# Segment 3's memory asked inside the attention, and the fallback flag ahead of the last halvings

## The chip, the cores and the metric

The kernel runs on one core of a Trainium2 chip. The metric is the device time of one execution in microseconds; a shorter time is better. The engines are TensorE (PE, with its weight loads shown apart as PEld), VectorE (DVE), ScalarE (ACT), GpSimd (POOL) and SyncE (SP, which here mainly issues DMAs). Work passes through SBUF, matmul results through the PSUM banks.

## The reference

Two attentions over 2048 tokens with a width of 576 and 32 heads of 18, whose outputs stand side by side. A has one key and one value head for all its query heads. B works in four segments of 512 tokens: a causal softmax inside the segment, and beside it a memory M, z of all the earlier segments, which is asked with phi(q).

```
phi = lambda t: jnp.where(t > 0, t + 1.0, jnp.exp(t))
# A
p = softmax(einsum("bhqd,bkd->bhqk", q, k) * Dh ** -0.5);  o = einsum("bhqk,bkd->bhqd", p, v);  out_A = o @ wo
# B, for s in range(4)
a_dot = einsum("bhqk,bhkd->bhqd", softmax(qs @ ks * scale + mask), vs)
num = einsum("bhld,bhde->bhle", phi(qs), M)
den = einsum("bhld,bhd->bhl", phi(qs), z)[..., None] + 1e-6
o = g * num / den + (1.0 - g) * a_dot          # g = sigmoid(beta), by head
M = M + einsum("bhld,bhle->bhde", phi(ks), vs);  z = z + sum over l of phi(ks)
out_B = concat of all o, @ wo
```

## The kernel before

**Projections.** The first stage computes q, k and v, A's first and then B's segments one by one (`for s in range(NSEG)`). A projection splits its fp32 operands into a high and a low part and adds the three products that matter: 14 matmuls of 512 columns for one part of 126 rows (`proj`, L249), and 14 of 288 or 306 columns for 128 tokens of v (`values`, L491). Parts t = 0 to 4 cover the 576 columns. q and k are then halved again (`split2`, a cast on ACT at L118 and a subtraction on DVE at L119) and stored to DRAM; v goes to DRAM through `vch`, copied by ACT (L493) and stored from ACT's DMA queue (L496, `vB`). The engines' order in this stage is set by a scheduler, within what `hold` and `pin` fix.

For each part of q in segments 1 to 3 `phi` (L382 to L389) runs a Relu and an Exp on ACT (L385, L386) and one max-and-add on DVE (L388). `from_memory(t)` (L423) then does one of two things. For a segment that is not in `LATE_ASK` it multiplies with the memory of the earlier segments on PE (L429), scales by the gate on DVE (L433) and stores `numB` (L434). For a segment in `LATE_ASK` it only stores phi(q) to `qfB` (L426). The denominators are formed in the same loop for segments that are not in `LATE_ASK`: five matmuls with `zst` (L545), 1e-6 added on DVE (L549), a store of `denB` (L550). `LATE_ASK` is (1, 2), so segment 3 asks inside its projections.

The scores' softmax has no running maximum; a bound for every query is subtracted instead. The bound's products stand at L554, its maximum in `fm` at L555, its halves in `shift_parts`. In the last segment `loose_flag` (L391 to L400) reduces all bounds to one number (a reduction on DVE, a transpose on PE at L396, another reduction, a comparison, a cast) and writes `flag`, which is 1 if a bound is too loose for fp32. The flag is loaded into registers of all engines (L606), and a branch (L607) leads either to a slow block, which isn't taken with these inputs, or past it. SP waits in the branch for DMAs that are still under way.

**Attention.** From there on a schedule written out by hand sets the order on PE, ACT and DVE (`tc.manual_schedule`). It is a list of 416 turns of three score items each (two, once in a block of A). An item is one tile of keys for two heads: matmuls into a PSUM tile `E` (L925 for A, L934 for B), an exp on ACT into `P` (L943), for one item of three by way of a copy `W` on DVE (L940); for some items of A the exp is computed on DVE (L898 to L908). The products with v, `O` (L973), follow two turns behind. A block of A has 11 turns, a block of B two; after each of the first blocks of A come two or four blocks of B. Between scores and products a turn has a place for one other piece of PE work:

- while `ask_memory` lasts (from turn k = 20 on, `ASK`), a step of it in turns whose items are all of A: four matmuls of 256 columns (L827), 12 steps to a segment, with the scaling (L832), the 1e-6 (L836) and stores of `numB` and `denB` behind them. The memories of all late segments are loaded together from `mzB` into the tile of A's output weights (L810), the phi(q) of one segment by `load_qf` (L802) into one of two "o" tiles;
- once it has ended, one step of an output projection: `run_fill(1)`, eight matmuls of 192 columns (L770). What isn't done by the last turn is done behind it, in the tail (L1133 on).

Loads, sums, inverses, weightings and stores hang on a list of due turns (`at`, `due`): `finish` begins a block's sums, `place()` (L1056) tells when the parts of another block may take an "o" tile: fewer than two in use, and the late segments asked so far at least `min(2, len(parts) + 1)`. Stacks of queries and keys (`stA`, `stB`, L138, L139) come by SP's queue two ahead.

Of the kernel before, what the change touches and what calls it, by code (L numbers as in the profile page):

```python
# [54 lines left out]
CA = 618  # L55
MZ = 126 + 32

LATE_ASK, ASK = (1, 2), 20


def below(rows, r0):
# [10 lines left out]
def attention_pair_kernel(ctx, tc, a_xT, a_w, a_wo, b_xT, b_w, b_wo, b_beta, ident_d, hmask_d, bmask_d, cmask_d, sel_d, zmask_d, selx_d, sely_d, out):  # L72
    nc = tc.nc
# [40 lines left out]
    def split2(pool, src, R, hold=lambda ins: ins):  # L114

        n = src.shape[-1]
        qp = pool.tile([128, 2, C], F32R, name="qp", bufs=3)
        hold(nc.scalar.copy(qp[:R, 0, :n], src))  # L118
        hold(nc.vector.tensor_tensor(qp[:R, 1, :n], src, qp[:R, 0, :n].bitcast(F32), op=ALU.subtract))  # L119
        return qp  # L120
# [32 lines left out]
    with ExitStack() as ph:  # L153
# [30 lines left out]
        pin = tc.keep_in_program_order  # L184
# [217 lines left out]
        for s in range(NSEG):  # L402
# [15 lines left out]
            def magnitude(t, pj):  # L418
                R = RT[t]
                aqs[t] = p2.tile([128, C], BF, name="aq", bufs=5)  # L420
                nc.scalar.activation(aqs[t][:R], pj[:R], AF.Abs)

            def from_memory(t):  # L423
                R = RT[t]
                if s in LATE_ASK:
                    nc.sync.dma_start(qfB[s][:R, t], fs[t][:R])  # L426
                    return
                pn = ps.tile([128, C], F32, name="mm", bufs=1)
                nc.tensor.matmul(  # L429
                    pn[:R], Mst[:R, t].rearrange("p h d -> p (h d)")[:, :R], fs[t][:R], start=True, stop=True  # L430
                )
                nm = p2.tile([128, C], F32, name="nm", bufs=2)
                nc.vector.tensor_scalar(nm[:R], pn[:R], gt[:R, t : t + 1], None, op0=ALU.mult)  # L433
                nc.sync.dma_start(numB[s][126 * t : 126 * t + R], nm[:R])  # L434
# [88 lines left out]
            if not last:  # L523
                for i in range(4):
                    values(i, 1)

            for t in range(4):
                pj = ps.tile([128, C], F32, name="pj", bufs=4)
                proj(pj[:126], wBh, wBl, xh, xl, 126 * t, 126)
                magnitude(t, pj)  # L530
                qp = split2(pt, pj[:126], 126)
                store_parts(qp, 0, 126, qB[s], 7 * t, 7)
                if s == 0:
                    nx[2](t, behind=True)
                    if t == 3:
                        nx[2](4, behind=True)
                if s:
                    fs[t] = phi(pj[:126], 126, "qf", 5)
                    from_memory(t)
# [15 lines left out]
            nc.vector.tensor_reduce(fm[:, 1 + s : 2 + s], pu, axis=AX.X, op=ALU.max)  # L555
            if last:
                loose_flag()
            sp = shift_parts(pt, pu, -BOUND_UP, C, 128)
            sent = nc.sync.dma_start(shB[s].rearrange("j r t -> r j t"), sp.bitcast(F32))
            if last:  # L560
# [241 lines left out]
    def load_qf(s):  # L802
        qfs[s] = pa.tile([128, 5, C], F32, name="o", bufs=2)
        nc.sync.dma_start(qfs[s][:126, :4], qfB[s][:126, :4])
        nc.sync.dma_start(qfs[s][: RT[4], 4], qfB[s][: RT[4], 4])
# [210 lines left out]
    def at(k, cost, ready, step):  # L1016
        later.append((k, cost, ready, step))
        later.sort(key=lambda e: e[0])
# [15 lines left out]
    def finish(k, ab, c, hg):  # L1034

        ts = range(4) if hg == 6 else range(4, 5)
        lo, hi = (0, 28) if hg == 6 else (28, 32)
        box, need = {}, 3 if ab == "B" and c > 0 else 1
        weighed.setdefault((ab, c), 0)
        last = (ab, c) == blocks[-1][:2]  # L1040

        d0, d1, d2, d3 = (0, 2, 0, 3) if last else (2, 5, 3, 5) if (ab, c) == ("B", 0) else (2, 5, 3, 6)

        def begin(k):
            assert ab == "A" or c not in LATE_ASK or asked[0] >= c
            summing.add(hg)
            box[0] = sums(ab, c, lo, hi)
            at(k + d1, 0, lambda: True, inv)

        def inv(k):  # L1050
            inverses(ab, c, lo, hi, box[0])
            summing.remove(hg)
            for t in ts:
                at(k, 0, place, lambda k, t=t: load(k, t))

        def place():  # L1056

            return (ab, c) in parts or len(parts) - filled[0] // FILL < 2 and asked[0] >= min(2, len(parts) + 1)

        def load(k, t):  # L1060
            load_heads(ab, c, t)
            at(k + d2, 0, room, lambda k: weights(k, t))

        def room():

            return loaded[0] + need <= 10

        def weights(k, t):
            loaded[0] += need
            tiles = load_inverses(ab, c, t)  # L1070
            box[t, t] = weigh(ab, c, t, tiles)
            at(k + d3, 1, lambda: True, lambda k: heads(k, t))

        def heads(k, t):
            box[t, t].pop(0)()
            if box[t, t]:
                at(k, 1, lambda: True, lambda k: heads(k, t))
                return
            loaded[0] -= need
            weighed[ab, c] += 1  # L1080
            if weighed[ab, c] == 5 and not last:
                at(k + 2, 0, lambda: True, lambda k: fill.append(out_proj(ab, c)))

        at(k + d0, 0, lambda: hg not in summing, begin)
# [8 lines left out]
    with tc.manual_schedule(engines={ENG.PE, ENG.Activation, ENG.DVE}):  # L1093

        for n, b in enumerate(blocks):
            ms = [m for m in range(len(its)) if block_of[m] == n]
            items = [(m, k) for m in ms for k in range(2)]
            for out_, cut in ((turns, len(items) // 3), (prods, len(items) // 3 - 2)):  # L1100
                at_ = split(len(items), cut)
                out_ += [items[a:z] for a, z in zip(at_, at_[1:])]
        at(ASK + 4, 0, lambda: True, lambda k: load_qf(2))
        for k in range(len(turns) + 2):
            now[0] = k
            exps = [scores(its[n], pr, i == 1) for i, (n, pr) in enumerate(turns[k])] if k < len(turns) else []
            for i in (0, 2, 1) if len(exps) == 3 else range(len(exps)):
                exps[i]()
            if memory is None:
                run_fill(1)  # L1110
            elif k >= ASK and all(its[n][0] == "A" for n, pr in turns[k]) and next(memory, None) is None:
                memory = None

            ends = k > 1 and any(hf and its[n][3] == (NKT - 1 if its[n][0] == "A" else 2) for n, hf in prods[k - 2])
            if slow and (slow[0][0] <= k or not ends):
                slow.pop(0)[2]()
            for n, hf in prods[k - 2] if k > 1 else []:
                ab, c = its[n][:2]
                hg = products(its[n][:3], its[n][3], hf)
                if hg in (6, 7):  # L1120
                    finish(k, ab, c, hg)
                if hg == 7 and ab == "B" and c + 1 < NSEG:
                    load_vseg(c + 1)
            due(k)
            for n, pr in turns[k] if k < len(turns) else []:
                it = its[n]
                ab = it[0]
                if pr == 0:
                    prefetch(ab, keys[ab].index((ab, it[1], it[2] // 2)) + 2)
                    if it in (("A", 0, 2, 8), ("A", 0, 5, 8)):  # L1130
                        load_wo(*(("B", b_wo) if it[2] == 2 else ("A", a_wo)))

        ab, c = blocks[-1][:2]  # L1133
        ending.append(True)
        while fill:
            due(k, 4)
            run_fill(8, whole=True)
            k += 1
        while weighed[ab, c] < 4:
            due(k, 4)  # L1140
            k += 1
        banks = [psE.tile([128, 2, 512], F32, name="E") for _ in range(3)]
        dst = [bk[:, hf, :288] for bk in banks for hf in range(2)]
        for nm in ("O", "F"):
            bk = psO.tile([128, C], F32, name=nm)
            dst.append(bk[:, :288])
        for g in range(8):
            for t in range(4):
                out_part(ab, c, g // 2, t, dst[g], 288 * (g % 2), 288, t == 0, False)
        while later:  # L1150
            due(k, 4)
            k += 1
        for g in range(8):
            out_part(ab, c, g // 2, 4, dst[g], 288 * (g % 2), 288, False, True)
        for i in range(4):
            osb = pp.tile([128, 2, 512], F32, name="P", bufs=PBUFS)
            for hf in range(2):
                (nc.vector.tensor_copy if hf else nc.scalar.copy)(osb[:, hf, :288], dst[2 * i + hf])
            out_store(ab, c, i, osb[:, :, :288])
# [56 lines left out]
```

## Time and profile before

| | |
|---|---|
| median of 3 runs | 1428.27 us |
| lowest and highest | 1426.28 and 1429.96 us |
| the profiled execution | 1427.14 us |
| its span, first to last instruction | 1425.4 us |
| busy in the span: PE, ACT, DVE, POOL | 1410.3, 1195.2, 1022.9, 247.0 us |
| mean granted TensorE clock | 0.997 |

"Busy" is the time in which at least one instruction of an engine ran; matmuls overlap, so PE's busy time isn't PE at its peak. The projections take the span up to about 290 us, the attention lasts to about 1376 us, and the rest is the tail. Times in rows count from the span's start. A row of a timeline or a chain starts with the time and the length in us; brackets give how long the engine sat idle before, and what released it.

### The profile page before, as it was taken

To read this page: it belongs to the slowest core of one execution; us is meant where nothing else is said; L and a number is where in the kernel's file an instruction comes from. 1 tells how busy PE (TensorE), PEld (TensorE's weight loads), DVE (VectorE), ACT (ScalarE), POOL (GpSimd) and SP (SyncE) were. 2 spreads that over 40 slices of the span, in tenths; PEclk is the share of its full clock that TensorE was granted. 3 is DMA by queue.
4 is the path that set the end of the run, shared out by engine and by line. 5 is a ranking of instruction groups with operands and counts; after the bars stand their busy time and mean duration, and the time that the engine had idled before them with its cause. 6 is when DMAs were issued, how large, how long until landed. Compare 5 with 4: busy or idle time off the path is not lost.

```text
span 1425.4 us, 41103 instructions
## 1 busy us (share of the span) xinstructions
PE 1410.3 (99%) x17692; PEld 839.5 (59%) x17692; DVE 1022.9 (72%) x1213; ACT 1195.2 (84%) x1429; POOL 247.0 (17%) x326
## 2 busy tenths in 40 slices
PE   9999999999999999999999999999999999999998
PEld 6788888755555555555555555555555555555565
DVE  6556456467787778777777888777778877877761
ACT  4543434489999999999999999999999999999960
POOL 2431000003313214131111150131013300200001
PEclk9999999999999999999999999999999999999999
DMA  9866546457564535232322532231105121110022
GB/s 275 261 215 188 168 143 226 161 165 230 158 202 159 170 109 175 87 108 77 102 68 66 175 118 86 85 114 64 36 34 151 48 78 51 51 43 18 18 87 77
DMA packets 90469, 172.71 MB, mean 121 GB/s; under 512 B 14576, under 2 KB 22377, under 8 KB 89854
## 3 DMA queue, kind: packets, MB, share of 16 engines
q1 hardware_dynamic: 83722, 159.75, 35.8%
q0 software_dynamic: 1664, 4.78, 1.3%
q10 hardware_dynamic: 4896, 5.51, 1.2%
q8 instruction: 140, 2.29, 0.7%
q14 instruction: 47, 0.39, 0.1%
HBM read 99.32 MB, written 70.67 MB: 119 GB/s over the span
## 4 chain that ended last, share of the span: by engine, by line
PE 66%; ACT 9%; issue 2%; DVE 1%; DMA 0%; POOL 0%; DVEq 0%; ACTq 0%
PE O L973 30%; PE E L925 19%; PE F L770 11%; ACT P L943 9%; PE E L934 3%; PE E L770 1%; PE F L827 1%; PE O L770 1%; DVE W L940 1%; DMA out<-osb 0%; DVE osb L795 0%; DVE q L905 0%; DVE q L902 0%; POOL P L948 0%; DVE o L832 0%
## 5 line engine op out<-in xcount | busy, mean ns | idle before, releaser
L943 ACT ACTIVATE P<-E 128x1024 f32<-128x1024 f32 (+1 forms) x800 | 783.3, 1065 | 12.1 <-PE E L925 12.0
L940 DVE COPY W<-E 128x1024 f32<-128x1024 f32 (+1 forms) x384 | 461.2, 1201 | 177.9 <-PE E L925 120.6
L973 PE MATMUL O<-P,VA 128*32 128x256 f32 x7936 | 508.5, 380 | 0.0
L943 ACT ACTIVATE P<-W 128x1024 f32<-128x1024 f32 (+1 forms) x384 | 429.1, 1117 | 2.4 <-DVE W L940 2.2
L973 PEld LDWEIGHTS O<-P,VA 128*32 128x32 f32 x7936 | 262.7, 110 | 146.5 <-issue 5.7
L925 PE MATMUL E<-stA,kstA 56*128 56x512 f32 x1920 | 328.4, 439 | 1.1 <-ACT P L943 0.4
L925 PEld LDWEIGHTS E<-stA,kstA 56*128 56x128 f32 x1920 | 154.9, 184 | 176.3 <-ACT P L943 110.2
L948 POOL TENSOR_SCALAR_AFFINE_SELECT P<-P 128x256 f32<-128x256 f32 (+1 forms) x192 | 94.6, 493 | 474.4 <-ACT P L943 441.5
L758 POOL TENSOR_TENSOR o<-o,rb 126x512 f32<-126x512 f32 (+1 forms) x55 | 81.2, 1490 | 410.7 <-PE F L770 142.2
L770 PE MATMUL F<-woB,o 126*32 126x192 f32 (+1 forms) x1920 | 127.4, 338 | 0.3 <-DVE osb L795 0.3
L905 DVE SCALAR_TENSOR_TENSOR q<-q,PD 128x1024 f32<-128x1024 f32 x96 | 119.3, 1243 | 0.0
L973 PE MATMUL O<-P,vseg 128*32 128x256 f32 (+2 forms) x1536 | 81.4, 344 | 0.0
L770 PEld LDWEIGHTS F<-woB,o 126*32 126x32 f32 (+1 forms) x1920 | 38.2, 108 | 70.8 <-issue 62.4
L770 PE MATMUL F<-woA,o 126*32 126x192 f32 (+1 forms) x1240 | 77.7, 338 | 0.6 <-DVE osb L795 0.6
L982 DVE COPY oe<-O 128x512 f32<-128x512 f32 x64 | 44.3, 692 | 42.6 <-PE O L973 41.2
L118 ACT CAST qp<-pj 126x512 fp32r<-126x512 f32 (+1 forms) x54 | 30.9, 584 | 49.9 <-DVE kmB L447 32.7
L249 PE MATMUL pj<-xh,wBl 128*126 128x512 f32 x180 | 72.3, 403 | 0.0
L249 PE MATMUL pj<-xh,wBh 128*126 128x512 f32 x180 | 71.8, 400 | 0.0
L119 DVE TENSOR_TENSOR qp<-pj,qp 126x512 fp32r<-126x512 f32 (+1 forms) x54 | 36.6, 686 | 37.3 <-ACT qp L118 37.2
L934 PE MATMUL E<-stB 56*128 56x256 f32 (+3 forms) x512 | 61.7, 348 | 1.6 <-ACT P L943 1.1
L973 PEld LDWEIGHTS O<-P,vseg 128*32 128x32 f32 x1536 | 48.8, 109 | 24.3 <-issue 1.6
L934 PEld LDWEIGHTS E<-stB 56*128 56x128 f32 x512 | 38.6, 185 | 32.0 <-ACT P L943 22.3
(182 smaller groups left out, 1366.3 us busy)
## 6 DMA issues: line engine op xcount, KB each, us to landing
stB<-kB SPq DMA_DIRECT2D x96, 144.0 KB
stB<-qB SPq DMA_DIRECT2D x32, 288.0 KB
stA<-qA SPq DMA_DIRECT2D x30, 288.0 KB
oA<-oe SPq DMA_DIRECT2D x32, 256.0 KB
oB<-oe SPq DMA_DIRECT2D x32, 256.0 KB
qA<-qp SPq DMA_DIRECT2D x16, 504.0 KB
kB<-qp SPq DMA_DIRECT2D x16, 504.0 KB
qB<-qp SPq DMA_DIRECT2D x16, 504.0 KB
```

Of the source, the lines that this page charges most:

```text
L119: hold(nc.vector.tensor_tensor(qp[:R, 1, :n], src, qp[:R, 0, :n].bitcast(F32), op=ALU.subtract))
L249: nc.tensor.matmul(dst, w[:, c0 : c0 + M], x, start=i == 0, stop=i == len(ops) - 1)
L758: return lambda: tc.keep_in_program_order(nc.gpsimd.tensor_tensor(dst, a, b, op=op))
L770: nc.tensor.matmul(dst[32 * j : 32 * j + 32], parts[ab, c][: RT[t], t, r0 : r0 + 32], wo[ab][: RT[t], t, c0 : c0 + n], start=start, stop=stop,
L905: steps.append(lambda a=a: v.scalar_tensor_tensor(q, q, a, p, op0=ALU.add, op1=ALU.mult))
L925: nc.tensor.matmul(e[:, j], kstA[rows, 128 * kt : 128 * kt + 128], st[rows, h, :], start=True, stop=True)
L934: nc.tensor.matmul(e[:, j, c0 : c0 + 512 - 128 * k], st[rows, 4 + h, ks], st[rows, h, 128 * k :], start=True, stop=True)
L940: nc.vector.tensor_copy(src[:, :, :n], e[:, :, :n])
L943: nc.scalar.activation(p[:, :, :n], src[:, :, :n], AF.Exp, scale=SCALE)
L948: nc.gpsimd.affine_select(diag, diag, pattern=[[0, 2], [0, m], [1, 128]], base=0, channel_multiplier=-1, compare_op=ALU.is_ge, fill=0.0)
L973: nc.tensor.matmul(o[32 * j : 32 * j + 32, q0 : q0 + n], v, p[:, j % 2, p0 : p0 + n], start=m == hf == 0, stop=last and hf == 1,)
L982: nc.vector.tensor_copy(osb, o)
```

## The change

`LATE_ASK` takes in segment 3. So its memory is stored to `mzB` behind segment 2, its phi(q) is stored (now on GpSimd's queue in the last segment), and its numerators and denominators come from twelve more steps of `ask_memory`. `load_qf(3)` stands at the due turn 32, once segment 1 has been asked. A step of `ask_memory` now also stands in a turn of B if the products of that turn, two behind, are of B too. `place()` waits until three segments are asked for a second block's parts. `mzB` and its load grow by half.

In the last segment the halvings, stores, phis and `from_memory` of parts 2 and 3 are kept back in `rest` and run behind `loose_flag`, pinned in that order.

```diff
-LATE_ASK, ASK = (1, 2), 20
+LATE_ASK, ASK = (1, 2, 3), 20
...
             def from_memory(t):
                 R = RT[t]
                 if s in LATE_ASK:
-                    nc.sync.dma_start(qfB[s][:R, t], fs[t][:R])
+                    (nc.gpsimd if last else nc.sync).dma_start(qfB[s][:R, t], fs[t][:R])
                     return
...
+            rest = []
             for t in range(4):
                 pj = ps.tile([128, C], F32, name="pj", bufs=4)
                 proj(pj[:126], wBh, wBl, xh, xl, 126 * t, 126)
                 magnitude(t, pj)
+                if last and t > 1:
+
+                    rest.append((t, pj))
+                    continue
                 qp = split2(pt, pj[:126], 126)
...
             if last:
                 loose_flag()
+                for t, pj in rest:
+                    qp = split2(pt, pj[:126], 126, pin)
+                    store_parts(qp, 0, 126, qB[s], 7 * t, 7)
+                    fs[t] = phi(pj[:126], 126, "qf", 5, pin)
+                    from_memory(t)
...
         def place():
 
-            return (ab, c) in parts or len(parts) - filled[0] // FILL < 2 and asked[0] >= min(2, len(parts) + 1)
+            return (ab, c) in parts or len(parts) - filled[0] // FILL < 2 and asked[0] >= min(3, len(parts) + 2)
...
         at(ASK + 4, 0, lambda: True, lambda k: load_qf(2))
+        at(ASK + 12, 0, lambda: asked[0] >= 1, lambda k: load_qf(3))
...
-            elif k >= ASK and all(its[n][0] == "A" for n, pr in turns[k]) and next(memory, None) is None:
+            elif k >= ASK and its[turns[k][0][0]][0] in ("A", its[prods[k - 2][0][0]][0]) and next(memory, None) is None:
+
                 memory = None
```

## The prediction

> **What bounds the kernel now.** I read the table of windows first, cut at the borders of stages and of blocks of turns; then the last projection stage by line, the way from it to the attention, and the chain of waits inside the attention. In the windows the columns are the stretch and its length, then busy time (and instructions) of PE, PEld, DVE, ACT and POOL, the granted clock, the DMA share and GB/s.
>
> ```profile
> 260.58:290.28 29.70, 29.70 (x148) 20.70 (x145) 15.60 (x28) 13.68 (x27) 0.00 (x0) 1.00 0.58 195
> 290.28:291.83 1.55, 0.01 (x1) 0.03 (x1) 0.00 (x0) 0.40 (x1) 0.00 (x0) 1.00 0.07 14
> 292.87:299.70 6.83, 6.08 (x37) 2.64 (x36) 6.54 (x6) 6.83 (x8) 0.43 (x1) 0.50 0.44 102
> 339.38:368.72 29.34, 29.26 (x404) 14.81 (x400) 25.13 (x26) 29.00 (x32) 1.63 (x3) 1.00 0.63 189
> 368.72:387.24 18.52, 18.06 (x260) 10.56 (x256) 11.44 (x12) 18.51 (x24) 10.19 (x22) 1.00 0.53 164
> 455.74:475.21 19.47, 19.47 (x325) 12.23 (x321) 11.41 (x14) 19.47 (x26) 10.55 (x22) 1.00 0.33 91
> 601.17:630.32 29.15, 28.86 (x405) 14.92 (x402) 23.83 (x24) 29.11 (x32) 6.54 (x4) 1.00 0.42 133
> 1373.98:1425.40 51.42, 45.91 (x920) 31.46 (x916) 8.83 (x21) 4.92 (x8) 6.37 (x5) 0.97 0.25 85
> ```
>
> The last segment's projections (first row) are bound by PE: busy for all 29.70 us. A gap of 1.55 us follows, and then the attention, where ACT is busy for 29.00 of 29.34 us in A turns with memory steps, 18.51 of 18.52 in eight B turns that carry no other PE work, and 29.11 of 29.15 in A turns with output-projection steps ("fill"). So ACT's exps set its pace, with one near exception: in eight B turns with fill, PE and ACT are both full and the stretch is 0.95 us longer. The tail (last row) is PE's. It follows that PE time taken out ahead of the attention counts in full, as far as the way into the attention shortens with it, and that PE time put into the attention costs only what sticks out beyond ACT. The program lasts 1427.14 us in this execution, 1.74 more than its span of 1425.4; the median of the runs shown, 1428.27, is 1.13 above it.
>
> **The change, part by part.**
>
> *1. Less PE work in the last segment.* With segment 3 among those asked late, its five memory products (L429) go, and so do the five products of the denominators (L545), which are computed only for segments that are asked early. The groups by line of 260.5 to 292 (busy, then mean ns of one) and two rows of the timeline:
>
> ```profile
> L429 PE MATMUL mm<-qf,Mst 126*126 126x512 f32 (+1 forms) x10 | 5.2, 602 | 0.0
> L545 PE MATMUL nd<-qf,zst 126*32 126x512 f32 (+1 forms) x10 | 3.4, 602 | 0.0
> ...
> 283.14 1.02 PE L429 MATMUL mm<-qf,Mst 126*126 126x512 f32 x2
> 284.10 1.05 PE L545 MATMUL nd<-qf,zst 126*32 126x512 f32 x4
> ```
>
> One product is two records of 602 ns. Two L429 records take 1.02, so the second starts 0.42 behind the first; four L545 take 1.05, so 0.15 apart. PE pipelines, so what a group occupies is its pitch: ten L429 at 0.42 are 4.2 us, ten L545 between 0.15 and 0.42 are 1.5 to 4.2. I take 2.3 for these (the busy 3.4 less the 0.35 to 0.45 by which each of three groups overlaps its neighbours). Together 6.5. The new order costs some of it back: by its buffers the second of the last four values products uses the PSUM bank of the first and must wait for ACT's copy of it; I put that bubble at 0.5, from the 0.40 us of such a copy (below). So PE ends the projections **6.0 us** earlier, at about 284.3 instead of 290.28 (bounds 4.5 and 7.5).
>
> The DVE scalings (L433), the +1e-6 (L549) and the stores of numB and denB go with it; none was late for PE. In their place come five stores of phi(q) on POOL's queue, which issues no other transfer there.
>
> *2. The flag.* The halvings and phis of parts 2 and 3 move behind the flag's reduction.
>
> ```profile
> L400 DVE CAST flag<-fm x1: 141/141/141, 286.5 to 286.5; 1x1 int32<-1x1 f32 x1
> L606 DVEq TENSOR_LOAD <-flag x1: 1151/1151/1151, 286.7 to 286.7; - x1
> L607 SPq EVENT_SEMAPHORE  x8: 17/17/17, 291.1 to 291.6; - x8
> ...
> L386 ACT ACTIVATE ph_e<-ph_e 126x512 f32<-126x512 f32 x3 | 1.9, 628 | 0.1
> ...
> 288.89 0.33 ACTq L496 DMA_DIRECT2D vB<-vch  x1
> 290.32 0.40 ACT L493 COPY vch<-pj 128x288 f32<-128x288 f32 x1 [1.47 <-PE pj L491]
> 291.53 0.33 ACTq L496 DMA_DIRECT2D vB<-vch  x1
> 291.83 1.17 PE L925 MATMUL E<-st,kstA 56*128 56x512 f32 x6 [1.55 <-SPq L607]
> 292.57 1.02 ACT L943 ACTIVATE P<-E 128x1024 f32<-128x1024 f32 x1 [1.85 <-PE E L925]
> ```
>
> The flag was cast at 286.55, 3.7 us before PE's end, so it was not what held the attention. What ended last is SP's row: eight waits passed between 291.1 and 291.6, each for stores still under way, and PE's first E waited for SP. The youngest such store is the third of vB, issued at 288.89, so it took some 2.2 us to land; the fourth, at 291.53, lies behind the branch. In the changed program's order ACT loads the flag only behind the deferred phis, and **the fourth store comes ahead of the branch**: copy 284.35 to 284.75, store at about 284.85. The way from the youngest store to the first E was 291.83 - 288.89 = 2.94, so E at 287.8 and the first exp, 0.74 later, at 288.5. The other thing that could end last is DVE: behind the last phi's exps (behind the last copy ACT has a relu and an exp left, 0.63 each, to about 286.0) stands its max-and-add, some 0.7, to 286.7, then the flag's load of 1.15: 287.8 as well, an estimate from these rows. So the first exp comes at 288.5 instead of 292.57: **-4.1 us**. Bounds: -4.6 if the 0.5 us of SP's waits go by while the store lands, -2.4 if the store takes 3.9 us, as a POOL transfer below, in place of 2.2. The gap on PE grows from 1.55 to some 3.5 us.
>
> *3. Loads behind the branch.* Five POOL stores of 252 KB gate SP's next load of stB and POOL's clearing of vseg.
>
> ```profile
> wr<-b_w POOLq DMA_DIRECT2D x4, 252.0 KB, 3.9
> ...
> 295.66 0.31 SPq L138 DMA_DIRECT2D stB<-qB  x1
> ```
>
> The last one is issued at about 287 and lands near 291 (3.9 us, as a POOL load of that size), no later than stB would be sent anyway (295.66 - 4.1 = 291.6); its first reader is the first B turn, whose eight end at 339.38, where the window of A turns begins. I cost it at nothing, with over 20 us of cover; without that, 2 us once.
>
> *4. Twelve more memory steps.* The new condition also puts steps into B turns whose products are B's too. By the order of the changed program the 36 steps stand in turns 20 to 29, 32 to 48 and 51 to 59 (the kernel's k); new are eight B turns (32 to 37, 51, 52) and four A turns (56 to 59). Fill starts two turns later, and turns 119 and 120, which had none left, now have it: 354 turns with fill in both programs and 66 steps left for the tail, so the tail is unchanged. The chain that ended last, in order of time (start, length, what):
>
> ```profile
> 343.06 0.57 PE F L827 x8
> ...
> 346.06 1.30 PE O L973 x24
> 347.36 0.89 PE E L925 x6
> 348.24 0.57 PE F L827 x8
> 348.81 1.30 PE O L973 x24
> ...
> 464.43 0.46 PE F L770 x8
> 464.89 0.98 PE O L973 x24
> 465.87 0.83 PE E L934 x5
> 466.70 0.46 PE F L770 x8
> 467.17 1.19 PE O L973 x24
> 468.36 0.78 PE E L934 x10
> ...
> 469.60 0.98 PE O L973 x24
> ```
>
> An A turn with a memory step is 348.81 - 346.06 = 2.75 us: at ACT's floor (32 exps in 29.00 are 0.906 each, three of them 2.72). So the four A turns cost some 0.1 together, and the two late fill turns as much. Two B turns without other work take 18.52/4 = 4.63. With fill they take 469.60 - 464.89 = 4.71, all of it PE; a memory step is 0.57 - 0.46 = 0.11 longer, so with memory 4.93: 0.30 per pair over what is there now. Four pairs: at most 1.2, or 4 x 0.46 = 1.8 if the whole stretch of 455.74 (0.24 per pair) is the better row; at least 0, if PE's lead in finished E tiles carries it. PE can be ahead by up to one finished tile, an exp of 0.9 us, at the start of each of the two runs of B turns; I let it carry 0.7 of the 1.2 and take 0.5. Sum of this part: 0.5 + 0.1 + 0.1 = **+0.7 us** (0 to +2.0).
>
> *5. Larger tables.* Two more stores of mzB behind segment 2, and a load of half as much again (790 KB before).
>
> ```profile
> woA<-mzB SPq DMA_DIRECT2D x1, 790.0 KB
> ...
> 325.15 0.36 SPq L810 DMA_DIRECT2D woA<-mzB  x1
> ...
> SPq L148 <- DMA o<-qfB: 6.5, 2, 6.0
> SPq L984 <- DMA o<-qfB: 4.0, 1, 4.0
> ```
>
> The load was issued at 325.15 and its first step ran at 343.06, 17.9 us later. Half as much again is 1185 KB, 6.3 us at the 189 GB/s of the fourth window: inside that. SP was held for 6.0 and 4.0 us by loads of qf, at no loss that PE or ACT shows in these windows. Nothing, or 1 us if the queue is fuller.
>
> **Sum**: -4.1 + 0.7 = -3.4 (-4.6 to -0.4). That is 1423.7 against the profiled 1427.14, and **1424.9** against the median of 1428.27.
>
> **The rivals.**
>
> *R1, the way in shortens with PE.* If the store lands faster and DVE isn't late, the first exp moves by the whole 6.0 us less the 0.5 of SP's waits, and the B turns' memory steps vanish in ACT's shadow, which leaves 0.2 of part 4: -5.5 + 0.2 = -5.3, 1423.0; to -6.8 with the upper bound of part 1. For it: ACT is full in every B row. Against: the landing of 2.2 us now follows the last store.
>
> The clock bears on this.
>
> ```profile
> 300.54 1.94 ACT L943 ACTIVATE P<-E 128x1024 f32<-128x1024 f32 x2 [0.30 <-PE E L925]
> ```
>
> Behind the gap of 1.55 us stood 6.83 us at a granted clock of 0.50, and ACT lost only this 0.30 us by it, at its end. The Trainium skill, "TensorE: Matmul & The Clock Gate", Part 1 (The HAM clock gate), has the clock fall after at least one idle window of about 3.4 us. Here 1.55 us was enough, so the row decides, and I leave the half clock in; by the page's rule a gap shorter than its window would keep the full clock, and the sum would be 0.3 us better.
>
> *R2, a longer half clock.* If the longer gap gives three windows of half clock instead of two (6.83/2 = 3.4 us each), PE falls behind in the third: an A turn has 1.30 + 0.89 = 2.2 us of PE by the chain's rows, 4.4 at half clock, where ACT needs 2.72, so ACT loses 3.4 x (1 - 2.72/4.4) = 1.3 us; with the memory steps at their +2.0 the sum is -4.1 + 1.3 + 2.0 = -0.8: 1427.5. For it: the gap doubles. Against: the half clock lasted the same two windows' length behind a gap of less than half of one.
>
> *R3, SP's queue is blocked by the third asking: slower.* Three segments share two "o" buffers. The load of qf3 waits until the stores of segment 1 have left its buffer, and SP stands before it; the two rows above show SP held for 6.0 and 4.0 us at qf loads. Each such wait holds back every stA and stB load behind it, and from where a hold exceeds the lead of these loads, PE waits as long as the excess. The third asking adds three holds (its load, its numB, its denB store); at 4.0 each, with the lead used up by the first two, they cost 12.0, and the sum is -3.4 + 12.0 = +8.6: 1436.9. Against: at those holds PE and ACT were full in the windows around them, so the lead was more than 6.0.
>
> *R4, it doesn't do what it says*: the fill that starts two turns later isn't made up, and lengthens the tail by two steps of 0.46 us. The sum becomes -2.5: 1425.8. The equal counts of fill turns speak against it.
>
> **How the numbers follow.** 0.3% of 1428.27, about what a measurement of this kernel can tell from no change, is 4.3 us: faster is below 1424.0, slower above 1432.6. My forecast has 0.61 (with its own bounds -4.6 to -0.4), of it 0.19 faster and 0.42 within, since -3.4 lies 0.9 short of the line and the gate's bound just beyond it; R1 0.17, faster; R2 0.09 and R4 0.02, within; R3 0.11, slower. That is 0.36 faster, 0.53 within, 0.11 slower. The range holds the forecast, R1 to -6.8, R2 and R4: 1421.5 to 1428.8, the last 0.9 beyond the forecast's upper bound of -0.4 for the unknown cost of part 5; R3 is left out, and a little at either end.
>
> **What would show it.** Right: PE's last projection near 284.3; the fourth vB store ahead of the branch; first exp near 288.5; turns 32 to 37 at 4.9 a pair; tail of 51.4. Wrong: PE's first E held by DVE or SP beyond 288.5 (R2); granted clock 0.50 for over 7 us (R2) or not at all (R1); B pairs at 4.65 (R1); PE waiting for a DMA in the turns after 32 (R3); a tail above 51.9 (R4).

## The result and the profile after

The changed kernel takes 1436.49 us (median of 5 runs, 1435.04 to 1437.32) where the kernel before takes 1428.62 (5 runs, 1426.28 to 1429.96): 1.0052 times as long, 95% interval 1.0038 to 1.0066. It is slower by some 7.5 us, and the time lies outside the range that was given. The profiled execution took 1436.63, with a span of 1434.9, which is 9.5 longer than that of the kernel before.

The windows of the changed kernel, with the columns as before. The first three rows are the end of the projections, the gap and the start; then B's turns 30 to 37, the turns 46 and 47, and the tail.

```profile
260.58:284.43 23.85, 23.36 (x126) 18.52 (x124) 10.62 (x21) 12.35 (x25) 2.18 (x4) 1.00 0.63 206
284.43:291.15 6.72, 0.61 (x2) 0.21 (x2) 0.69 (x1) 1.53 (x3) 0.53 (x1) 0.80 0.76 229
291.15:299.21 8.06, 7.70 (x41) 3.34 (x41) 6.54 (x6) 7.18 (x8) 0.14 (x1) 0.53 0.38 88
367.94:387.67 19.73, 19.65 (x308) 11.90 (x305) 13.92 (x16) 19.56 (x25) 10.73 (x23) 1.00 0.53 165
409.32:423.65 14.33, 8.37 (x80) 3.98 (x76) 8.99 (x12) 6.44 (x8) 0.00 (x0) 0.76 0.70 220
1383.76:1434.90 51.14, 45.85 (x920) 32.47 (x916) 8.81 (x21) 4.91 (x8) 6.36 (x5) 0.97 0.25 86
```

PE ends the projections at 284.43, as forecast, and 5.85 us earlier than before. Almost nothing comes of it: the gap is 6.72 us instead of 1.55, and the granted clock is 0.50 from 288.41 to 298.65, nearly to the end of the third row. In turns 46 and 47 PE is busy for 8.37 of 14.33 us; such turns take 2.77 each otherwise. Taken turn by turn against the kernel before, the start of the fourth turn is 0.78 ahead, that of turn 32 as much, turn 41 only 0.20, turn 48 is **8.61 behind**, and the last turn 9.8 behind; the tail gives 0.3 back. One place makes nearly all of the loss: turns 41 to 47, with 8.8 us.

What happened there is in the chain of the changed kernel (start, length, what; "DMA" is the time from a transfer's issue to its landing):

```profile
389.81 4.64 DMA numB<-o
...
394.53 0.33 SPq L814
...
394.90 0.39 SPq L815
...
395.34 7.59 DMA stA<-qA
...
402.94 9.94 DMA sm<-oB
...
412.91 0.96 DVE sm L736
...
414.10 1.23 DVE W L950
...
415.37 0.81 PE E L935 x2
```

and in its waits from 400 to 425 (who, for what: us in total, times, longest):

```profile
ACT P L953 <- DVE W L950: 6.4, 2, 5.9
DVE sm L736 <- DMA sm<-oB: 5.7, 1, 5.7
PEld E L935 <- DVE W L950: 5.7, 1, 5.7
PE E L935 <- DVE W L950: 5.3, 1, 5.3
```

Read it from the end. PE had no free E bank, for DVE had not copied one into W; DVE stood at the reciprocal of B's first sums (L736), which the schedule places in turn 46 ahead of that copy; and the sums' load `sm`, issued at 402.94, landed at 412.88. In the kernel before it was issued at 396.26, and DVE, which came to the reciprocal at 407.3, didn't wait for it:

```profile
396.26 0.86 SPq L713 DMA_DIRECT2D sm<-oB  x1
...
L726 DVE RECIPROCAL sm<-sm x2: 241/594/947, 407.3 to 414.9; 112x128 f32<-112x128 f32 x1, 128x16 f32<-128x16 f32 x1
```

Ahead of it now stands the new load of segment 3's phi(q) (L814, L815), for which SP waited until the first memory store, numB, had landed. In both kernels SP sends `sm` only when the stack stA has landed. Of the 6.7 us by which `sm` is late, 4.4 come from stA's later issue (395.34 for 390.98) and 2.3 from its slower landing, 7.59 us for 5.28.

PE's wait itself is 5.3 of the 8.8 us. Behind it the granted clock is 0.50 from 414.71 to 421.53, and matmuls that take 1.30 us at full clock take 2.56:

```profile
417.88 2.56 PE O L983 x24
...
422.43 1.30 PE O L983 x24
```

The gap at the start, by SP's row for the branch:

```profile
L617 SPq EVENT_SEMAPHORE  x8: 17/17/17, 284.4 to 291.3; - x8
...
281.32 2.95 SPq L123 DMA_DIRECT2D qB<-qp  x2
...
284.90 0.33 ACTq L496 DMA_DIRECT2D vB<-vch  x1
291.15 1.61 PE L935 MATMUL E<-st,kstA 56*128 56x512 f32 x5 [2.31 <-SPq L617]
291.95 4.05 ACT L953 ACTIVATE P<-E 128x1024 f32<-128x1024 f32 x4 [5.92 <-PE E L935]
```

The fourth vB store is issued at 284.90, as forecast (284.85). But SP's fifth wait passes only at 290.89, and by its semaphore it belongs to the second of the two qB stores (L123), issued at 283.90: 7 us to land. It is the store of part 3's halves, which the change moved behind the flag. The sixth wait, by its semaphore that for the fourth vB store, passes at 291.17. That is 0.28 later, where the waits behind it follow 0.07 apart, so this store seems to have landed last, 6.3 us after its issue. The first exp comes at 291.95 instead of 292.57.

### The profile page after: what moved, and what is told of

Read it like the earlier page. It is cut to its first block, busy times and chain, and to the rows that moved or that the text cites. A ratio compares the mean times of both kernels' runs of the same rounds, so it can differ in the third digit from the quotient of the medians.

```text
span 1434.9 us, 41259 instructions
## 1 busy us (share of the span) xinstructions
PE 1410.6 (98%) x17768; PEld 842.2 (59%) x17768; DVE 1023.2 (71%) x1214; ACT 1195.6 (83%) x1429; POOL 251.6 (18%) x331
## 4 chain that ended last, share of the span: by engine, by line
PE 66%; ACT 7%; issue 2%; DMA 2%; DVE 1%; SPq 0%; POOL 0%; DVEq 0%; ACTq 0%
PE O L983 30%; PE E L935 19%; PE F L780 11%; ACT P L953 7%; PE E L944 3%; PE E L780 1%; PE F L837 1%; DMA sm<-oB 1%; DMA stA<-qA 1%; PE O L780 1%; DVE W L950 0%; DMA rA<-sm 0%; DMA out<-osb 0%; DMA numB<-o 0%; DVE osb L805 0%
## 5 line engine op out<-in xcount | busy, mean ns | idle before, releaser
L768 POOL TENSOR_TENSOR o<-o,rb 126x512 f32<-126x512 f32 (+1 forms) x55 | 84.6, 1556 | 370.7 <-DMA o<-oA 144.8
L249 PE MATMUL pj<-xl,wBh 128*126 128x512 f32 x144 | 57.3, 399 | 0.0
```

The source lines that it names most:

```text
L249: nc.tensor.matmul(dst, w[:, c0 : c0 + M], x, start=i == 0, stop=i == len(ops) - 1)
L768: return lambda: tc.keep_in_program_order(nc.gpsimd.tensor_tensor(dst, a, b, op=op))
```

## The experiments

The theories. For the stall: **Q**, SP's queue is held at the store, so `sm` is issued late; **B**, the bytes of the new load stand ahead of `sm` in the DMA queues, wherever it is issued from; **D**, whatever makes it late, only DVE's reciprocal stops PE. For the start: **G**, the moved qB store alone; **M**, the bytes that are still to be stored; **H**, POOL's stores; **L**, each late store's own time to land. Times are medians, beside the runs of the kernel before on the same chip.

At 100 us of the span, where none of the edits has changed anything yet, the traces already stand up to 2.9 us apart. So at the start of the attention times are best counted from PE's end of the projections. Six profiles have the changed kernel's projections: its own, and those of the runs with phi(q) on another queue, phi(q) later, the reciprocal later, `vseg` later, and of the last control. In them the first exp comes 6.6 to 8.2 us behind PE's end (7.5 in the changed kernel), the fourth turn 14.5 to 16.0 (14.8), and the fourth vB store lands 5.6 to 6.9 us after its issue (6.3).

**The new load on another queue**

```diff
-        nc.sync.dma_start(qfs[s][:126, :4], qfB[s][:126, :4])
-        nc.sync.dma_start(qfs[s][: RT[4], 4], qfB[s][: RT[4], 4])
+        q = nc.gpsimd if s == 3 else nc.sync
+        q.dma_start(qfs[s][:126, :4], qfB[s][:126, :4])
+        q.dma_start(qfs[s][: RT[4], 4], qfB[s][: RT[4], 4])
```

> The changed kernel, with the load of segment 3's phi(q) on GpSimd's queue instead of SyncE's. In the changed kernel PE stood still from 409 to 415 us: DVE waited 5.75 us for the sums' load sm, issued by SP 6.6 us later than before, behind a wait of SP for the numB store to land (389.8 to 394.5). Theory Q (SP's queue is held): sm is issued near 397 again, the stall of 8.3 us goes, and the time falls to about 1428. Rival B (bytes: the DMA queues carry 1 MB more at that time): the same bytes at the same time, sm lands near 412 again, and the time stays within 2 us of 1436.5.

1438.35 (before 1427.91; ratio 1.0074, 1.0055 to 1.0093). The hold is gone, `sm` is issued at 398.35, and it still lands at 413.31, by the chain of this run:

```profile
393.27 5.06 DMA stA<-qA
...
398.35 14.96 DMA sm<-oB
...
413.33 0.96 DVE sm L736
```

Q alone falls. A load of 56 KB took 14.96 us, behind 1216 KB of `vseg` (issued at 396.33) and 1152 KB of phi(q) (395.02, from the other queue): at the 236 GB/s that the DMA moved in the changed kernel from 402.9 to 412.9, these two alone are 10.3 us, an estimate. The Trainium skill, "DMA: Bandwidth & Descriptors", section Queues, rings and completion order, says that the write which reports a transfer as done lands only after every earlier write of the same DMA engine, across its queues. This run agrees, since another queue did not help, but a rate that all the queues share would show the same.

**The new load later**

```diff
-        at(ASK + 12, 0, lambda: asked[0] >= 1, lambda k: load_qf(3))
+        at(ASK + 20, 0, lambda: asked[0] >= 1, lambda k: load_qf(3))
```

> The changed kernel, with the load of segment 3's phi(q) eight turns later (due turn 40 instead of 32), so that it stands behind the sums' load in SP's order. Theory Q: SP isn't held for the numB store, sm is issued near 397 and the stall at 409 goes; the phi(q) is then issued near 398 and may be up to 2 us late for its first step near 409; 1428 to 1430. Rival B: the bytes move behind sm too, so the stall goes by this theory as well; only the first experiment tells them apart, and this one shows whether the load has room for the delay.

1432.15 (1429.24 to 1436.32; ratio 1.0032, 1.0018 to 1.0045). In the profiled run `sm` is issued at 397.02, ahead of phi(q), and the loss from turn 41 to turn 47 is 1.2 us instead of 8.3. What is left there is PE's wait for phi(q), landed at 410.94:

```profile
PE F L837 <- DMA o<-qfB: 1.1, 1, 1.1
```

The load has no room for the delay. That the times spread over 7 us would fit a load which is late in some executions only; that isn't shown.

**The reciprocal later**

```diff
-        d0, d1, d2, d3 = (0, 2, 0, 3) if last else (2, 5, 3, 5) if (ab, c) == ("B", 0) else (2, 5, 3, 6)
+        d0, d1, d2, d3 = (0, 2, 0, 3) if last else (2, 9, 3, 5) if (ab, c) == ("B", 0) else (2, 5, 3, 6)
```

> The changed kernel, with the inverses of B's first block four turns later (due after 9 turns instead of 5), and nothing else. Theory D (what stops PE is only DVE's reciprocal, in order ahead of the copies W, waiting for sm; the late load itself hurts nobody): sm lands near 413 as before, DVE doesn't meet the reciprocal until about 424, and the stall goes: about 1428. Rival: something else behind SP's hold (the stack stA, landed at 402.9, or phi(q) for the step at 409) stops PE near the same time: PE still waits 4 us or more, above 1433.

1433.66 (1429.28 to 1437.62; ratio 1.0038, 1.0025 to 1.0052). From turn 41 to turn 52, where the changed kernel loses 9.2 us, this run loses 0.6. D is right: phi(q) and the stacks were there in time, and only the reciprocal in DVE's order stopped PE. The rest of the time comes from elsewhere: in the profiled run the projections are 2.2 us behind the changed kernel's from 90 us on, so that the fourth turn starts 1.3 behind the kernel before, and at turn 68 another 2.3 are lost to a late stack of B:

```profile
465.69 4.85 DMA stB<-ones_d
...
470.67 0.87 PE E L944 x4
```

**The bytes ahead of `sm`**

```diff
-                    load_vseg(c + 1)
+                    at(k + 6, 0, lambda: True, lambda k, c=c: load_vseg(c + 1))
```

> The changed kernel, with the load of the next segment's values (vseg, 1216 KB) six turns later, so that it stands behind the sums' load sm in the queues instead of ahead of it; phi(q)'s load stays where the change has it. Theory B (sm lands late because of the bytes ahead of it: the run with phi(q) on GpSimd's queue had sm issued at 398.35 and landed 14.96 us later): 1.2 MB less ahead, at 236 GB/s some 5 us, so sm lands near 407 to 408 instead of 412.9 and the stall of 8.3 us shrinks to 0 to 3: about 1428.5 to 1431. Theory Q (SP's hold alone): sm is issued at 401 to 402 as before and the stall stays near 8: about 1436.

1431.67 (before 1427.90; ratio 1.0028, 1.0017 to 1.0039). SP's hold stays: `sm` is issued at 402.04, once phi(q) has landed. It lands 3.5 us earlier than in the changed kernel:

```profile
395.86 6.16 DMA o<-qfB
...
402.04 7.33 DMA sm<-oB
...
409.39 0.96 DVE sm L736
```

DVE's wait falls from 5.7 to 1.3 us, and the loss from turn 41 to turn 48 from 8.8 to 3.6. So it is the bytes, and SP's hold adds its part: `sm` is still issued 5.8 us later than before the change.

**The halvings back ahead of the flag**

```diff
+                qp = split2(pt, pj[:126], 126)
+                store_parts(qp, 0, 126, qB[s], 7 * t, 7)
                 if last and t > 1:
                     rest.append((t, pj))
                     continue
-                qp = split2(pt, pj[:126], 126)
-                store_parts(qp, 0, 126, qB[s], 7 * t, 7)
...
                 for t, pj in rest:
-                    qp = split2(pt, pj[:126], 126, pin)
-                    store_parts(qp, 0, 126, qB[s], 7 * t, 7)
```

> The changed kernel, with only the phis of parts 2 and 3 behind the flag: the two halvings and the stores of their halves to qB are back ahead of it. In the changed kernel SP's drain wait passed at 290.89, with the semaphore of the qB store issued at 283.9 (7 us to land), and PE's second E came at 291.15. Theory G (that store is the gate): the waits pass with the last vB store, near 287.3 to 288, the first exp comes near 288.8 instead of 291.95 and the half clock ends earlier; the stall at 409 stays, so about 1433.5. Rival H (POOL's stores of phi(q) fill the DMA queues, so that whatever is last lands late): the last vB store lands as late, first exp at 291 or later, about 1436.

1435.56 (ratio 1.0049, 1.0031 to 1.0066). The first exp comes at 290.81, not 288.8: the last of the three qB stores is issued at 279.0, and now the third vB store, issued at 283.03, is the last to land, at 290.46. (The fourth is issued at 286.33, behind ACT's branch, so that one store fewer is waited for.) Counted from PE's end the first exp comes at 6.4 us, and at 5.9 and 6.7 in the two runs below that share this edit. G explains some 1 us of the gap at most; another store takes its place.

**All of it back ahead of the flag**: the rest list is left empty (`if False:` for `if last and t > 1:`).

> The changed kernel with the second half of the change undone: all halvings, stores and phis of the last segment ahead of the flag again, segment 3 still asked in the attention. Theory M: the same bytes as in the changed kernel, a little earlier, so the drain ends at 290 to 290.5, the first exp near 291, and the rest as in the changed kernel with its stall: about 1435. A rival in which the flag's order is what counts: the flag, 2 to 3 us later, holds the branch beyond 291.5 and the time is above 1437.

1436.09 (ratio 1.0056, 1.0037 to 1.0074). The first exp comes at 292.89, the waits pass by 292.28: 2 us later than M had it, of which 1.1 are this execution's later projections. Counted from PE's end the first exp comes at 7.3 us and the fourth turn at 14.8, as in the changed kernel. So the second half of the change gains nothing that these runs can tell, at the start or in the time. The waits pass between 287.3 and 292.3, long after the flag: it isn't the flag that holds the branch.

**Fewer bytes: no stores of phi(q)**

```diff
-                    (nc.gpsimd if last else nc.sync).dma_start(qfB[s][:R, t], fs[t][:R])
+                    if not last:
+                        nc.sync.dma_start(qfB[s][:R, t], fs[t][:R])
...
-        nc.sync.dma_start(qfs[s][:126, :4], qfB[s][:126, :4])
-        nc.sync.dma_start(qfs[s][: RT[4], 4], qfB[s][: RT[4], 4])
+        nc.sync.dma_start(qfs[s][:126, :4], qfB[min(s, 2)][:126, :4])
+        nc.sync.dma_start(qfs[s][: RT[4], 4], qfB[min(s, 2)][: RT[4], 4])
```

> The changed kernel without the stores of segment 3's phi(q); segment 3 asks with segment 2's phi(q) instead, so its memory part is left out in effect, while all loads and steps of the attention stay. In the changed kernel the DMA queues are 0.89 to 0.92 busy from 281 to 288, and SP's drain waits pass at 290.9 to 291.3; with the halvings put back ahead of the flag another store was the last one there, at 290.46. Theory M (the way into the attention is now bound by the bytes still to be stored): 1.15 MB less at about 0.25 MB/us of the shared rate, of which three parts (0.75 MB) lie behind 278, bring the waits to 288 or earlier and the first exp to 288.5 to 289.3 (DVE's last phi and its load of the flag end near 288.1). Rival (the landing time of the late stores is their own, whatever else is under way): waits at 290.5 or later, first exp at 291.5 or later.

The first exp comes at 290.80. As the projections end 1.0 us later here, that is 5.4 us behind PE's end instead of 7.5. The wait for the fourth vB store passes at 290.52, 4.6 us after its issue, with the queues nearly empty from 289 on (DMA share 0.09). M had the direction, but its 288 was some 1.5 us too early. (One execution, 1436.82; the stall at turn 46 stays.)

**Fewer bytes still**: the run above, also without the stores of q's halves of parts 2 and 3.

```diff
                     qp = split2(pt, pj[:126], 126, pin)
-                    store_parts(qp, 0, 126, qB[s], 7 * t, 7)
...
-        load_q(st[:, 0:4], qB[s], 8 * h8)
+        load_q(st[:, 0:4], qB[min(s, 2)], 8 * h8)
```

> The run without the stores of segment 3's phi(q), and also without the stores of q's halves of parts 2 and 3 in segment 3: 2.15 MB less at the end of the projections; segment 3's scores and memory part use segment 2's q instead, all loads and steps of the attention stay. Theory M (the drain is bound by bytes): the queues are empty by 287, the waits pass there and the first exp comes at 288.5 to 289. Theory L (each late store takes its own time to be acknowledged, 4 to 6 us for the fourth store of vB as in the run with 1.15 MB less, where it was issued at 285.92 and the last wait passed at 290.52): waits again at 289.5 or later, first exp at 290 or later.

```profile
284.00:286.00 2.00, 0.20 (x2) 0.00 (x0) 0.17 (x1) 1.53 (x3) 0.00 (x0) 1.00 0.46 155
286.00:288.00 2.00, 1.20 (x6) 0.69 (x6) 0.52 (x1) 0.00 (x0) 0.00 (x0) 0.92 0.03 9
288.16:297.13 8.97, 6.31 (x36) 2.61 (x37) 6.54 (x6) 7.66 (x8) 0.14 (x1) 0.50 0.43 100
...
L617 SPq EVENT_SEMAPHORE  x8: 17/17/17, 283.1 to 288.2; - x8
```

The DMA share is 0.46 and then 0.03, where the changed kernel shows 0.90 from 284 to 288; the wait for the fourth vB store, issued at 284.67, passes at 287.89, and the first exp comes at 288.31. That is near the 288.5 of the forecast, which held for empty queues, though partly by chance: the store took 3.2 us where the forecast had 2.2, but the first E, at 286.80, no longer came behind the waits. L falls, as the same fourth store landed 3 us sooner. It takes 6.3, 4.6 and 3.2 us as 0, 1.15 and 2.15 MB are left out, so M is right as a whole. POOL's stores (H) are a part of these bytes; no run shows them as a cause of their own. (One execution, 1433.34; the stall stays.) The last row shows a second price: the start still takes 8.97 us at half clock, and of the 4.3 us that the first exp gains over the kernel before 2.9 are left at the fourth turn.

**The queue edits and the halvings together**: `vseg` six turns later, phi(q) at `ASK + 20`, halvings ahead of the flag.

> The changed kernel with three edits together: the load of vseg six turns later, phi(q)'s load at due turn 40 behind sm, and the halvings and stores of parts 2 and 3 back ahead of the flag (only the phis stay behind it). If theory B and the bytes of the drain are all that is wrong: no stall near 409, the start 1 us better than in the changed kernel, the B turns' memory steps still at their +1.2: about 1426 to 1428.5, level with the kernel before or a little faster. Rival: phi(q) is late for its first step (PE waits at about 409 for the DMA by 1 us or more), or vseg is late for B's second segment near 420: above 1430.

1427.79 (1426.17 to 1431.28) against 1427.90; ratio 1.0006, 0.9994 to 1.0018: no different from the kernel before. There is no wait for `sm`; the loss from turn 41 to turn 47 is 0.75.

**The same without memory steps in B turns**: the last edit of the change undone.

```diff
-its[turns[k][0][0]][0] in ("A", its[prods[k - 2][0][0]][0])
+all(its[n][0] == "A" for n, pr in turns[k])
```

> The combination of the last call (vseg six turns later, phi(q) of segment 3 at due turn 40, halvings ahead of the flag), with the kernel before's rule for the turns of memory steps: none in turns with an item of B. In the combination the six steps in turns 32 to 37 cost 1.2 us net and those in 51, 52 some 0.4. Theory P (a memory step in a B turn is worth its price, since every turn that the asking lasts longer is a turn without output projection): B turns 30 to 37 take 18.5 again, the asking ends some 13 turns later, about ten steps of output projection of 0.46 us move to the tail, and the time is 1429.5 to 1432. Rival (the B turns' steps are a plain loss): the time is 1 to 2 us below the combination's 1427.8, 1426 to 1427.

1438.92 (before 1427.34; ratio 1.0075, 1.0058 to 1.0092). As P has it, turns 30 to 37 lose nothing any more, and the tail, from the start of the last turn, takes 56.3 us instead of the combination's 50.9. But in the profiled execution, the slowest of the four, 8.5 us more are lost from turn 65 to turn 69, where PE waits for a stack of B behind the later stores and loads. So the whole time is no measure of the steps' price; only the tail's 5.4 us is.

**Two controls**: the `vseg` edit on the kernel before, and the combination without the halvings' edit.

> The kernel before the change, with the load of vseg six turns later and nothing else: the control for the combination. In the kernel before, DVE's first reciprocal never waited for sm (issued at 396.26, met at 407.3), so by theory B there is nothing to win: 1427 to 1428.5. If the edit gains 2 us or more by itself, the combination's 1427.8 is that gain over a change that still loses.

> The changed kernel with the two edits for the queues (vseg six turns later, phi(q) of segment 3 at due turn 40), and the halvings of parts 2 and 3 behind the flag as the change has them: the combination without its third edit. By theory B no stall near 409. By the runs so far the halvings behind the flag cost some 1 us at the start (start of the fourth turn 0.8 us ahead of the kernel before, against 1.7 to 2.2 with them ahead of it): 1428 to 1430. If it is level with or below the combination, their place doesn't count.

The first gives 1429.02 against 1427.76 (ratio 1.0007, 0.9995 to 1.0020): the edit gains nothing by itself. The second gives 1429.12 (ratio 1.0010, 0.9999 to 1.0022): without a stall the change is back at the kernel before, and the difference to the combination is too small for these runs.

## Why the prediction was wrong

- *Less PE work* was right: 5.85 us earlier for 6.0. *Loads behind the branch* cost nothing, as forecast: the 0.78 us of the fourth turn are still there at turn 32.
- *The flag, and the way into the attention*, failed. The forecast took the youngest store, rightly it seems, as the last to land, and gave it the 2.2 us of the kernel before; it took 6.3. By the forecast's own part 1 the stores now had 6 us less to flow out in. From 284 to 288 the DMA share was 0.90 instead of 0.68, a store issued at 283.9 took 7 us, and the first exp gained 0.62 us instead of 4.1. DVE's way, put at 287.8, ended at 288.1 and was not what held. The qB stores that move with the halvings were not counted at all. With 2.15 MB fewer to store the forecast's time nearly came out, 288.31. (Of SP's eight waits in the kernel before only the first, at 291.12 for the third vB store, was still for a store under way; the others passed 0.06 to 0.09 apart behind it.)
- *The half clock* was left as it was. PE stood still for longer, the half clock began earlier (288.41 for 292.87), lasted 10.24 us instead of 6.83 and ended 1.05 earlier (298.65 for 299.70), so the fourth turn was 0.78 us ahead.
- *Twelve more memory steps* was mis-sized. The pairs of turns 32 to 37 cost 0.43, 0.62 and 0.16 us more than before and 51, 52 0.44: 1.65 for 1.2. As 0.63 of it came back in the turns of A behind the first three, 1.0 is left for the 0.5 that was taken. The tail was as forecast, 51.14 for 51.42.
- *Larger tables* is the step that made it wrong: "Nothing, or 1 us if the queue is fuller" was measured at 8.8 us, of which 5.3 are PE's wait and most of the rest is the half clock behind it. It weighed the mzB load, and saw in SP's holds that nothing waited. It did not add the 1152 KB of the third phi(q), 5.0 us at 236 GB/s, to a place where the queues of the kernel before were already full, nor ask which small load with a fixed consumer stood behind it. The window of the kernel before, then the next one of the changed kernel:

```profile
394.50:402.90 8.40, 8.40 (x122) 4.36 (x118) 8.06 (x8) 8.26 (x10) 0.00 (x0) 1.00 0.97 279
```

```profile
402.90:412.90 10.00, 7.15 (x100) 3.57 (x92) 4.26 (x5) 6.54 (x8) 0.00 (x0) 1.00 0.90 236
```

  The DMA share is 0.97 without the load; with it, 0.90 and longer, with PE idle for 2.85 of 10 us.
- *R3* named the side and the cause's first half, SP before the third load, and gave 1436.9. Its mechanism was not this one: three holds that use up the lead of the stacks. The runs show one stall, at DVE's reciprocal, made mostly by bytes; with the hold removed it stayed. That its price fits is chance.
- *R2* had the length of the half clock right: 10.24 us, three times 3.41. Its price of 1.3 us did not come, since the half clock began 2.7 us ahead of the second E: from the first exp to the fourth turn it took 7.26 us, and 7.42 before. *R1* and *R4* did not occur: the pairs of B turns cost more, and the tail did not.

Added up by turns: 0.8 gained at the start where 4.1 had been forecast, 1.0 for the memory steps, 8.8 in turns 41 to 47, and some 0.5 in small pieces, the tail counted in, make the 9.5 us by which the span grew.

## What to carry to other kernels

A transfer costs the ones behind it: before a megabyte is added, look at the DMA share of the stretch where it lands, and find the smallest load in it that an engine waits for in a fixed order. A small load is best issued ahead of a large one, and here another queue was no way round it. Where a stage ends by draining its stores, PE time taken out of it only lengthens the wait once the queues are full. And before the starts of two traces are compared, look whether the traces were level ahead of the edit.

## What had not been expected of the hardware

Where PE stood still for some 3 to 7 us between the stages, the length of the half clock varied from run to run: 10.24 us in most of the changed kernels, 13.65 in two, that with `vseg` later and the combination without the halvings' edit; 6.83 behind the 1.55 us of the kernel before. The second of the two has it, in its profiled run, from its first E to the fourth turn:

```profile
290.78:303.14 12.36, 8.95 (x42) 3.71 (x43) 6.54 (x6) 7.66 (x8) 0.14 (x1) 0.50 0.39 105
```

Its fourth turn starts 3.15 us behind that of the kernel before, where the combination's starts 2.21 ahead. Of these 5.4 us 2.8 are projections that ended later, and only the rest belongs to the gap and the clock: counted from PE's end, the fourth turns come at 16.0 and 13.4 us. The Trainium skill, "TensorE: Matmul & The Clock Gate", Part 1 (The HAM clock gate), says that the window over which the clock is decided runs freely and doesn't reset with the kernel; that would make a spread in the length, and no run here isolates it.

The half clock also prices a stall inside the attention. Wherever PE stood still at turn 46 by the full amount, 6.83 us at a granted clock of 0.50 followed; `vseg` later, with less of a stall, had 3.41 us of it, and the runs without the stall had none there.
